# One threshold for two tiles, earlier weights for the first batch, a start split on GpSimd, and more transposes by DMA, in an attention kernel with a dense layer behind it

## The chip, the cores and the metric

The kernel runs on one core of a Trainium2 chip. The metric is the device time of one execution in microseconds (us), the median of several runs. All runs told here are on one core. Ratios are the mean time of one kernel's runs over that of the other kernel's runs of the same rounds, so not quite the ratio of the medians that are quoted beside them. The interval after a ratio holds it with 95%.

## The reference

Eight batches of eight heads, 576 positions, head size 64. Each head keeps only the scores within tau of its row's maximum, applies a softmax to them and multiplies by v. The heads are put side by side (512 columns) and go through a dense layer.

```python
scores = scale * np.matmul(q, k.transpose(0, 1, 3, 2))
thresh = np.max(scores, axis=-1, keepdims=True) - tau
scores = np.where(scores >= thresh, scores, -1000000000.0)
...                                     # softmax over the row
attn_out = np.matmul(attn, v)
x = attn_out.transpose(0, 2, 1, 3).reshape(B * S, H * D)
h = x @ w_in                            # 512 -> 2048
y = (h - np.tanh(h)) @ w_out            # 2048 -> 512
```

## The kernel before

Two heads make a pair; 32 pairs, of nine tiles of 128 query rows each (tile 4 is a mixed one, with 64 rows of either head, called M). The kernel walks over 288 slots, one tile a slot (about 1.6 us each in the steady part). In slot s it makes the scores of tile s+7, the threshold of tile s+6 (`shift`), the mask of tile s+5 (`kink`, on ScalarE), the weights of tile s (`weights`, an exp on ScalarE) and the product with v of tile s-2. TensorE also carries the dense layer of the previous batch between the slots. The mask `z` has to be transposed before the exp. In the first two batches TensorE does that, afterwards a DMA transpose does (`dma_start_transpose`; "by DMA" below), with two tiles in one transfer. All DMAs of the steady part are issued in order by one queue, that of SyncE (SP). q and k have to be turned too, by TensorE for every pair.

```python
AHEAD, MASK, LAG = 7, 5, 2
NPE = 2 * HPAIR * TPP                    # tiles transposed on TensorE
sc_pool = pool("sc", AHEAD - MASK + 2)
...
def scores(i):
    ...                                  # eight matmuls into ps
    mx = st_pool.tile([P, 1], F32, name="mx", tag="mx")
    nc.vector.tensor_scalar(out=sc, in0=ps[:, lo : lo + S], scalar1=SC,
        scalar2=None, op0=ALU.mult, op1=ALU.max, accum_out=mx)

def shift(i):                            # the threshold of one tile
    nb = st_pool.tile([P, 1], F32, name="nb", tag="nb")
    nc.vector.tensor_scalar(out=nb, in0=mx, scalar1=-1.0, scalar2=tau,
                            op0=ALU.mult, op1=ALU.add)

def kink(i):                             # the mask, then its transpose
    nc.scalar.activation(out=z, in_=sc, func=ACT.Prelu, bias=nb,
                         scale=1.0, alpha=STEEP)
    if i < NPE:
        zts[i] = zt                      # TensorE will transpose it
    elif kd != "A":                      # A: first tile of two, B: second
        nc.sync.dma_start_transpose(out=zts[i][:, 0:n, :], in_=zt)
...
for s in range(-AHEAD, NTILE + LAG + 3):
    shift(s + AHEAD - 1); scores(s + AHEAD)      # (bounds left out)
    kink(s + MASK); weights(s)
    ...                                  # a share of the dense layer
    attend(s - LAG)
    for step in plan.pop(s, []): step()  # loads, splits, turns of later pairs
```

Of the kernel before, what the change touches and what calls it, by code (L numbers as in the profile page):

```python
# [18 lines left out]
def kernel(  # L19
# [34 lines left out]
    NPE = 2 * HPAIR * TPP  # L54
# [4 lines left out]
    MASK = 5  # L59
# [21 lines left out]
    for i in range(NV):  # L81
        vb = const.tile([P, 2, 6, D + 1], BF16, name=f"vb{i}")
        nc.gpsimd.memset(vb[:, :, 4:6, :], 0.0)
        nc.vector.memset(vb[:, :, 0:4, D : D + 1], 1.0)
        nc.vector.memset(vb[0:64, :, 4, D : D + 1], 1.0)
        nc.vector.memset(vb[64:P, :, 5, D : D + 1], 1.0)
        vbs.append(vb)
# [3 lines left out]
    for i in range(NM):  # L91
# [9 lines left out]
    fold = const.tile([P, 64], BF16, name="fold")  # L101
    nc.vector.tensor_tensor(
        out=fold, in0=ident_bf[:, 0:64], in1=ident_bf[:, 64:P], op=ALU.add
    )

# [82 lines left out]
    def split_first(t, part):  # L188
        cs = (slice(0, 5), slice(5, TPP))[part]
        r = raws[0, t][:, cs, :]  # L190
        if part == 0:
            hls[0, t] = hl_pool.tile([P, TPP, 2, D], FP16, name=f"{t}hl", tag=t)
        hl = hls[0, t][:, cs, :, :]
        nc.scalar.mul(out=hl[:, :, 0, :], in_=r, mul=QKSC)
        nc.vector.scalar_tensor_tensor(
            out=hl[:, :, 1, :], in0=r, scalar=QKSC, in1=hl[:, :, 0, :],
            op0=ALU.mult, op1=ALU.subtract,
        )
# [25 lines left out]

    def turn(p, t):
        hl = hls.pop((p, t))
        ps = ps_big.tile([P, W], FP16, name=f"ps_{t}", tag="big")
# [7 lines left out]
        if t == "k":  # L235
            sw = qk_pool.tile([P, W], FP16, name="kS", tag="ks")
            nc.gpsimd.tensor_copy(out=sw[0:D, :], in_=m[D:P, :])  # L237
            nc.gpsimd.tensor_copy(out=sw[D:P, :], in_=m[0:D, :])  # L238
            mats[p, "ks"] = sw
# [25 lines left out]
    scs, zs, zts, pts, ops = {}, {}, {}, {}, {}  # L265
# [5 lines left out]
    def scores(i):  # L271
# [6 lines left out]
        if j == 4:  # L278
            for n, kk in enumerate((kT, kS)):
                for dst, srcs in ((main, MAIN), (rem, REM)):  # L280
                    for hh in range(2):
                        nc.tensor.matmul(  # L282
                            out=ps[64 * hh : 64 * hh + 64, dst],
                            lhsT=qT[:, REM[hh]], rhs=kk[:, srcs[hh]],
                            start=(n == 0), stop=(n == 1),
                        )
        else:
# [9 lines left out]
        mx = st_pool.tile([P, 1], F32, name="mx", tag="mx")  # L297
        nc.vector.tensor_scalar(  # L298
            out=sc, in0=ps[:, lo : lo + S], scalar1=SC, scalar2=None,
            op0=ALU.mult, op1=ALU.max, accum_out=mx,  # L300
        )
        scs[i] = sc, mx

    def shift(i):
        sc, mx = scs[i]
        nb = st_pool.tile([P, 1], F32, name="nb", tag="nb")
        nc.vector.tensor_scalar(  # L307
            out=nb, in0=mx, scalar1=-1.0, scalar2=tau, op0=ALU.mult, op1=ALU.add
        )
        scs[i] = sc, nb  # L310

    def kink(i):
        sc, nb = scs.pop(i)
# [13 lines left out]
        if i < NPE:  # L327
# [6 lines left out]
    def weights(i):  # L334
# [4 lines left out]
        if i < NPE:  # L339
            z = zts.pop(i)  # L340
            ps = ps_y.tile([P, 5 * P], BF16, name="psZ", tag="y")
# [126 lines left out]
    def project(m, ms, part, ps, last):  # L468
        for n in range(4 * part, 4 * part + 4):
            nc.tensor.matmul(  # L470
                out=ps, lhsT=gs[m][:, n, ms * P : (ms + 1) * P],
                rhs=w_out_sb[:, n, :], start=(n == 0), stop=(n == DF_C - 1),
            )
        if part == 3:
            yo = y_pool.tile([P, d_model], F32, name="yo")
# [7 lines left out]
            else:  # L483
                for h in range(2):
                    b = 2 * ms + h
                    stores.append(
                        lambda b=b, h=h: nc.sync.dma_start(
                            out=out[b * S + MB : (b + 1) * S, :],
# [3 lines left out]

    def layers(m, tail):

        steps, cur = [], {}
# [8 lines left out]
        def y_step(ms, part):  # L504
            if part == 0:
                tag = ("y", "o")[ms % 2] if tail else "y"
                pl = {"y": ps_y, "o": ps_o}[tag]
                cur["y"] = pl.tile([P, d_model], F32, name="psY", tag=tag)
            project(m - 1, ms, part, cur["y"], tail and ms % 2)

        for a in range(16):
            if m < NMB:
                steps.append(lambda a=a: h_step(a))
            if m > 0:
                steps.append(lambda a=a: y_step(a // 4, a % 4))
        return steps

# [15 lines left out]
    def w_load(piece):  # L533
# [20 lines left out]
        (3, lambda p: turn(p, "q")),  # L554
# [4 lines left out]
    for p in range(1, NPAIR):  # L559
        first = TPP * p - AHEAD  # L560
        for d, f in PREP[3 if p == 1 else 0 :]:
            plan.setdefault(first - d, []).append(lambda p=p, f=f: f(p))

# [3 lines left out]
    for t in ("k", "q", "ks"):  # L567
        turn_first(t, 0)
    split_v(0)
# [5 lines left out]
    todo, stage = [], 0  # L575

    for at in sorted(plan):
        if at < -AHEAD:
            plan.setdefault(-AHEAD, []).extend(plan.pop(at))
    for s in range(-AHEAD, NTILE + LAG + 3):  # L580
# [10 lines left out]
        if s == 1 - AHEAD:  # L591
            for t in ("k", "q"):
                split_first(t, 1)
        if s == 2 - AHEAD:
            for t in ("k", "q", "ks"):
                turn_first(t, 1)
        if 0 <= s + MASK < NTILE:
            kink(s + MASK)
        bend()
        if 0 <= s < NTILE:  # L600
            weights(s)
            if todo:
# [3 lines left out]
                while todo and done >= 1:  # L606
                    todo.pop(0)()
                    done -= 1
        shrink()
# [3 lines left out]
        if 0 <= s - LAG < NTILE:  # L613
            attend(s - LAG)
            pp, jj = divmod(s - LAG, TPP)
            if jj == 4:
                norm(pp, 0)
            if jj == 8:
                norm(pp, 1)
        pp, jj = divmod(s - LAG, TPP)  # L620
        if jj == 1 and 0 < pp <= NPAIR:
            emit_x(pp - 1)
# [10 lines left out]
    while stage <= NMB:  # L633
# [45 lines left out]
```

## Time and profile before

| | before |
|---|---|
| median of 4 runs (first comparison) | 552.1 us (550.9 to 552.7) |
| median of the 11 runs beside each group of experiments | 551.6 us |
| profiled span | 549.4 us |
| busy share of TensorE, VectorE, ScalarE | 95%, 81%, 81% |
| ScalarE's wait for a transposed mask | none |

The exp of a transposed mask (`pT<-zT`) never found ScalarE (ACT) idle.

### The profile page before, as it was taken

The page shows a single profiled execution, that of the slowest core. Times are in us where ns is not written, and L with a number is a line of the kernel's source. Part 1 is how long each engine was busy: PE and PEld are TensorE (multiplying, and loading weights), DVE is VectorE, ACT ScalarE, POOL GpSimd, SP SyncE. Part 2 cuts the span into 40 slices and gives each one's busy share as a digit, 9 for nine tenths or more (in the row PEclk, how much of TensorE's full clock was granted, in tenths as well). Part 3 has the DMA queues.
Part 4 walks back from the last instruction along what each step waited for, and adds up shares of the span by engine and source line. Part 5 has one row for each costly group of instructions (what it writes and reads, how often), then busy time and mean ns, then how long its engine had stood idle before and what let it go on. Part 6 is the DMA issues. An engine that isn't in the chain of part 4 may idle for free.

```text
span 549.4 us, 13518 instructions
## 1 busy us (share of the span) xinstructions
PE 521.8 (95%) x4954; PEld 302.4 (55%) x4954; DVE 444.1 (81%) x1349; ACT 443.3 (81%) x640; POOL 286.5 (52%) x372
## 2 busy tenths in 40 slices
PE   5888999999999999999999999999999999999996
PEld 2566666665555555555555555555555555444442
DVE  5888988898988999898889898898989888544430
ACT  3999999899899898989888988989898989533320
POOL 6788977666556666556555655666665620000000
PEclk9999999999999999999999999999999999999999
DMA  6755644437879888889977798877878966310103
GB/s 168 216 183 146 205 125 145 128 74 157 161 153 172 178 181 160 169 171 170 186 174 173 165 182 164 167 180 179 163 169 171 185 87 144 66 39 38 40 38 78
DMA packets 183011, 80.33 MB, mean 146 GB/s; under 512 B 150688, under 2 KB 175264, under 8 KB 182944
## 3 DMA queue, kind: packets, MB, share of 16 engines
q1 hardware_dynamic: 182512, 79.17, 65.0%
q8 instruction: 39, 0.64, 0.5%
q10 hardware_dynamic: 432, 0.30, 0.2%
q14 instruction: 28, 0.23, 0.2%
HBM read 37.75 MB, written 9.44 MB: 86 GB/s over the span
## 4 chain that ended last, share of the span: by engine, by line
PE 72%; DVE 16%; ACT 8%; issue 2%; DMA 1%; SPq 0%; ACTq 0%; DVEq 0%
PE psY L470 20%; PE psH L444 18%; PE psS L292 15%; DVE sc L298 6%; PE psO L389 5%; ACT pT L352 4%; PE psS L282 3%; ACT z L324 3%; DVE g L463 3%; PE psHt L444 3%; PE ps_q L221 2%; PE ps_k L221 2%; PE psZ L343 2%; DVE yo L479 1%; DVE kT L233 1%
## 5 line engine op out<-in xcount | busy, mean ns | idle before, releaser
L298 DVE TENSOR_SCALAR_CACHE_REDUCE sc<-psS 128x576 f32<-128x576 f32 x288 | 216.3, 751 | 19.8 <-PE psS L282 12.5
L324 ACT ACTIVATE z<-sc,nb 128x576 bf16<-128x576 f32 x256 | 195.7, 769 | 14.3 <-DVE nb L307 13.4
L470 PE MATMUL psY<-w_out_sb,g 128*128 128x512 bf16 x576 | 145.4, 379 | 0.0
L360 ACT ACTIVATE pT<-zT 128x1152 f16<-128x1152 bf16 (+1 forms) x120 | 127.8, 1065 | 0.0
L444 PE MATMUL psH<-xT,w_in_sb 128*128 128x512 bf16 x480 | 124.0, 379 | 0.3
L292 PE MATMUL psS<-kT,qT 128*128 128x512 f16 (+1 forms) x512 | 105.2, 287 | 10.1 <-DVE nb L307 7.6
L292 PEld LDWEIGHTS <-qT 128*128 128x128 f16 x1024 | 75.5, 98 | 68.1 <-issue 15.9
L237 POOL COPY kS<-kT 64x1152 f16<-64x1152 f16 x31 | 35.3, 1140 | 141.4 <-DVE nb L307 141.4
L463 DVE SCALAR_TENSOR_TENSOR g<-th,psH 128x512 bf16<-128x512 f32 x128 | 87.4, 683 | 22.0 <-ACT th L457 22.0
L292 PE MATMUL psS<-kS,qT 128*128 128x512 f16 x496 | 101.4, 286 | 0.0
L457 ACT ACTIVATE th<-psH 128x512 f32<-128x512 f32 x128 | 74.7, 584 | 17.8 <-PE psH L444 17.6
L470 PEld LDWEIGHTS <-g 128*128 128x128 bf16 x576 | 49.6, 98 | 57.7 <-issue 2.6
L444 PEld LDWEIGHTS <-w_in_sb 128*128 128x128 bf16 x576 | 49.3, 98 | 55.0 <-issue 2.7
L389 PEld LDWEIGHTS <-pT 128*128 128x128 f16 x1280 | 55.6, 98 | 24.3 <-ACT pT L360 2.1
L389 PE MATMUL psO<-vb,pT 128*128 128x65 bf16 x1280 | 61.2, 193 | 0.6 <-ACT pT L360 0.6
L352 ACT ACTIVATE pT<-psZ 128x640 f16<-128x640 bf16 (+1 forms) x72 | 47.2, 656 | 6.9 <-PE psZ L343 6.2
L307 DVE TENSOR_SCALAR nb<-mx 128x1 f32<-128x1 f32 x288 | 42.6, 148 | 3.4
L324 ACT ACTIVATE zm<-sc,nb 128x576 bf16<-128x576 f32 x32 | 24.8, 774 | 23.1 <-DVE nb L307 23.1
L183 POOL TENSOR_TENSOR qhl<-xs,qhl 128x576 f16<-128x576 f32 x31 | 39.7, 1280 | 2.6
L183 POOL TENSOR_TENSOR khl<-xs,khl 128x576 f16<-128x576 f32 x31 | 39.7, 1279 | 2.6
L238 POOL COPY kS<-kT 64x1152 f16<-64x1152 f16 x31 | 35.4, 1142 | 1.3
L343 PE MATMUL psZ<-ident_bf,z 128*128 128x128 bf16 x288 | 26.5, 219 | 4.5 <-ACT pT L352 4.3
(72 smaller groups left out, 561.6 us busy)
## 6 DMA issues: line engine op xcount, KB each, us to landing
vraw<-in_v_dram SPq DMA_DIRECT2D x32, 256.0 KB, 3.5
out_dram<-yo SPq DMA_DIRECT2D x32, 256.0 KB, 2.6
kraw<-in_k_dram SPq DMA_DIRECT2D x31, 256.0 KB, 3.1
qraw<-in_q_dram SPq DMA_DIRECT2D x31, 256.0 KB, 3.2
wt<-in_moe_w_in_dram SPq DMA_DIRECT2D x8, 512.0 KB, 4.4
wt<-in_moe_w_out_dram SPq DMA_DIRECT2D x8, 512.0 KB, 3.9
vraw<-in_v_dram SPq DMA_DIRECT2D x64, 32.0 KB, 2.9
zT<-z SPq DMA_TRANSPOSE x96, 3.3
```

Source lines behind the costliest of these rows:

```text
L183: nc.gpsimd.tensor_tensor(out=hl[:, :, 1, :], in0=x, in1=hl[:, :, 0, :], op=ALU.subtract)
L292: nc.tensor.matmul(out=ps[:, dst], lhsT=lhs, rhs=kk[:, src], start=(n == 0), stop=(n == 1),)
L298: nc.vector.tensor_scalar(out=sc, in0=ps[:, lo : lo + S], scalar1=SC, scalar2=None, op0=ALU.mult, op1=ALU.max, accum_out=mx,)
L307: nc.vector.tensor_scalar(out=nb, in0=mx, scalar1=-1.0, scalar2=tau, op0=ALU.mult, op1=ALU.add)
L324: nc.scalar.activation(out=z, in_=sc, func=ACT.Prelu, bias=nb, scale=1.0, alpha=STEEP)
L352: nc.scalar.activation(out=pt[:, off * P : (off + n) * P], in_=ps[:, 0 : n * P], func=ACT.Exp)
L360: nc.scalar.activation(out=pt[:, 0 : n * P], in_=zts.pop(i)[:, 0:n, :], func=ACT.Exp)
L389: nc.tensor.matmul(out=po[:, (j - 1 - 5 * hh) + ab, :], lhsT=pt[:, blk * P : (blk + 1) * P], rhs=vb[:, hh, c, :], start=(n == 0), stop=(n ...
L444: nc.tensor.matmul(out=ps, lhsT=w_in_sb[:, c, n * P : (n + 1) * P], rhs=xs[m][:, c, :] if m < B else xR[:, c, :, :], start=(c == 0), stop= ...
L457: nc.scalar.activation(out=th, in_=ps, func=ACT.Tanh)
L463: nc.vector.scalar_tensor_tensor(out=gs[m][:, n, :], in0=th, scalar=-1.0, in1=ps, op0=ALU.mult, op1=ALU.add,)
L470: nc.tensor.matmul(out=ps, lhsT=gs[m][:, n, ms * P : (ms + 1) * P], rhs=w_out_sb[:, n, :], start=(n == 0), stop=(n == DF_C - 1),)
```

## The change

Its intent: take transposes off TensorE, which bounds the steady part (58.2 of 59.2 us busy in a stage), and shorten both ends of the run. It has six parts: (1) q of twelve odd pairs goes by DMA; (2) in the second batch half of the masks go by DMA; (3) one threshold instruction serves two tiles, and so the mask comes one slot later (`MASK` 4); (4) the first batch's weights come three slots sooner; (5) at the start, GpSimd splits the second half of k and q; (6) the layer steps are reordered, and the last columns are stored in halves. `MASK` 4 also gives the scores one more buffer (`sc_pool` above). Beside the six, the diff holds small moves: a few `memset`s on GpSimd, the first four masks and the turns of pair 1 at other slots, a second bank for the first batch's transposes, and q by DMA issued five slots ahead in place of three. The core of the diff, shortened:

```diff
-    NPE = 2 * HPAIR * TPP
+    def on_pe(i):
+        p, j = divmod(i, TPP)
+        return p < HPAIR or p < 2 * HPAIR and j in (0, 1, 4, 5, 6)
-    MASK = 5
+    MASK = 4
@@ split_first: the second half of k and q on GpSimd
+        else:
+            nc.gpsimd.tensor_scalar(out=r, in0=r, scalar1=QKSC, ...)
+            nc.gpsimd.tensor_copy(out=hl[:, :, 0, :], in_=r)
+            nc.gpsimd.tensor_tensor(out=hl[:, :, 1, :], in0=r, in1=hl[:, :, 0, :], op=ALU.subtract)
@@ turn
+    def q_by_dma(p):
+        return p >= 2 * HPAIR and p % 2 == 1
+        if t == "q" and q_by_dma(p):
+            m = mats[p, t] = qk_pool.tile([P, W], FP16, name=f"{t}T", tag=t)
+            nc.sync.dma_start_transpose(out=m.rearrange(...), in_=hl.rearrange(...))
+            return
@@ shift: one threshold for two tiles
-        nb = st_pool.tile([P, 1], F32, name="nb", tag="nb")
+        if kd == "A":
+            return
+        n = 2 if kd == "B" else 1
+        nb = st_pool.tile([P, 2], F32, name="nb", tag="nb")
         nc.vector.tensor_scalar(
-            out=nb, in0=mx, scalar1=-1.0, scalar2=tau, op0=ALU.mult, op1=ALU.add
+            out=nb[:, 0:n], in0=mx[:, 0:n], scalar1=-1.0, scalar2=tau,
+            op0=ALU.mult, op1=ALU.add,
@@ the loop: weights and products of the first batch three slots sooner
+        at = i - 3 if i < HPAIR * TPP else i
...                     (layer order, halves of the last columns: cut)
```

More of the change, by code (lines that the diff above doesn't have):

```diff
@@ L83 @@
         nc.gpsimd.memset(vb[:, :, 4:6, :], 0.0)
-        nc.vector.memset(vb[:, :, 0:4, D : D + 1], 1.0)
-        nc.vector.memset(vb[0:64, :, 4, D : D + 1], 1.0)
-        nc.vector.memset(vb[64:P, :, 5, D : D + 1], 1.0)
+        nc.gpsimd.memset(vb[:, :, 0:4, D : D + 1], 1.0)
+        nc.gpsimd.memset(vb[0:64, :, 4, D : D + 1], 1.0)
+        nc.gpsimd.memset(vb[64:P, :, 5, D : D + 1], 1.0)
         vbs.append(vb)
@@ L100 @@
     nc.vector.memset(own[64:P, 1, :], 1.0)
-    fold = const.tile([P, 64], BF16, name="fold")
-    nc.vector.tensor_tensor(
-        out=fold, in0=ident_bf[:, 0:64], in1=ident_bf[:, 64:P], op=ALU.add
-    )
     pool = lambda name, bufs, **kw: ctx.enter_context(
@@ L193, in split_first @@
         hl = hls[0, t][:, cs, :, :]
-        nc.scalar.mul(out=hl[:, :, 0, :], in_=r, mul=QKSC)
-        nc.vector.scalar_tensor_tensor(
-            out=hl[:, :, 1, :], in0=r, scalar=QKSC, in1=hl[:, :, 0, :],
-            op0=ALU.mult, op1=ALU.subtract,
-        )
+        if part == 0:
+            nc.scalar.mul(out=hl[:, :, 0, :], in_=r, mul=QKSC)
+            nc.vector.scalar_tensor_tensor(
+                out=hl[:, :, 1, :], in0=r, scalar=QKSC, in1=hl[:, :, 0, :],
+                op0=ALU.mult, op1=ALU.subtract,
+            )
+        else:
+            nc.gpsimd.tensor_scalar(
+                out=r, in0=r, scalar1=QKSC, scalar2=1.0, op0=ALU.mult, op1=ALU.mult
+            )
+            nc.gpsimd.tensor_copy(out=hl[:, :, 0, :], in_=r)
+            nc.gpsimd.tensor_tensor(
+                out=hl[:, :, 1, :], in0=r, in1=hl[:, :, 0, :], op=ALU.subtract
+            )
     def split_v(p):
@@ L223, in turn_chunk @@
         )
+    def q_by_dma(p):
+        return p >= 2 * HPAIR and p % 2 == 1
     def turn(p, t):
         hl = hls.pop((p, t))
+        if t == "q" and q_by_dma(p):
+            m = mats[p, t] = qk_pool.tile([P, W], FP16, name=f"{t}T", tag=t)
+            nc.sync.dma_start_transpose(
+                out=m.rearrange("p (c r) -> p c r", c=TPP),
+                in_=hl.rearrange("p c a d -> p (c a d)"),
+            )
+            return
         ps = ps_big.tile([P, W], FP16, name=f"ps_{t}", tag="big")
@@ L236, in turn @@
             sw = qk_pool.tile([P, W], FP16, name="kS", tag="ks")
-            nc.gpsimd.tensor_copy(out=sw[0:D, :], in_=m[D:P, :])
-            nc.gpsimd.tensor_copy(out=sw[D:P, :], in_=m[0:D, :])
+            for lo, hi in ((0, D), (D, 0)):
+                o, i = sw[lo : lo + D, :], m[hi : hi + D, :]
+                nc.gpsimd.tensor_copy(out=o, in_=i)
             mats[p, "ks"] = sw
@@ L264 @@
     REM = (slice(512, 576), slice(576, 640))
-    scs, zs, zts, pts, ops = {}, {}, {}, {}, {}
+    scs, mxs, nbs, zs, zts, pts, ops = {}, {}, {}, {}, {}, {}, {}
     def kind(j):
@@ L278, in scores @@
         if j == 4:
+            qrem = REM
+            if q_by_dma(p):
+                qrem = (slice(512, 640, 2), slice(513, 640, 2))
             for n, kk in enumerate((kT, kS)):
@@ L283, in scores @@
                             out=ps[64 * hh : 64 * hh + 64, dst],
-                            lhsT=qT[:, REM[hh]], rhs=kk[:, srcs[hh]],
+                            lhsT=qT[:, qrem[hh]], rhs=kk[:, srcs[hh]],
                             start=(n == 0), stop=(n == 1),
@@ L296, in scores @@
         sc = sc_pool.tile([P, S], F32, name="sc")
-        mx = st_pool.tile([P, 1], F32, name="mx", tag="mx")
+        if kind(j) == "B":
+            mx = mxs[i] = mxs.pop(i - 1)
+        else:
+            mx = mxs[i] = st_pool.tile([P, 2], F32, name="mx", tag="mx")
+        c = int(kind(j) == "B")
         nc.vector.tensor_scalar(
             out=sc, in0=ps[:, lo : lo + S], scalar1=SC, scalar2=None,
-            op0=ALU.mult, op1=ALU.max, accum_out=mx,
+            op0=ALU.mult, op1=ALU.max, accum_out=mx[:, c : c + 1],
         )
-        scs[i] = sc, mx
+        scs[i] = sc
     def shift(i):
-        sc, mx = scs[i]
-        nb = st_pool.tile([P, 1], F32, name="nb", tag="nb")
+        kd = kind(i % TPP)
+        if kd == "A":
+            return
+        n = 2 if kd == "B" else 1
+        mx = mxs.pop(i)
+        nb = st_pool.tile([P, 2], F32, name="nb", tag="nb")
         nc.vector.tensor_scalar(
-            out=nb, in0=mx, scalar1=-1.0, scalar2=tau, op0=ALU.mult, op1=ALU.add
-        )
-        scs[i] = sc, nb
+            out=nb[:, 0:n], in0=mx[:, 0:n], scalar1=-1.0, scalar2=tau,
+            op0=ALU.mult, op1=ALU.add,
+        )
+        nbs[i] = nb[:, n - 1 : n]
+        if kd == "B":
+            nbs[i - 1] = nb[:, 0:1]
     def kink(i):
-        sc, nb = scs.pop(i)
+        sc, nb = scs.pop(i), nbs.pop(i)
         kd = kind(i % TPP)
@@ L326, in kink @@
         )
-        if i < NPE:
+        if on_pe(i):
             zts[i] = zt
@@ L338, in weights @@
         n, off = {"A": (4, 0), "M": (5, 0), "B": (5, 4)}[kd]
-        if i < NPE:
+        if on_pe(i):
             z = zts.pop(i)
-            ps = ps_y.tile([P, 5 * P], BF16, name="psZ", tag="y")
+            pl, tag = (ps_h, "h") if i % 2 and i < HPAIR * TPP else (ps_y, "y")
+            ps = pl.tile([P, 5 * P], BF16, name="psZ", tag=tag)
             for c in range(n):
@@ L466, in shrink, with project @@
             )
-    def project(m, ms, part, ps, last):
+    def project(m, ms, part, ps, last, cols=slice(0, d_model)):
         for n in range(4 * part, 4 * part + 4):
@@ L471, in project @@
                 out=ps, lhsT=gs[m][:, n, ms * P : (ms + 1) * P],
-                rhs=w_out_sb[:, n, :], start=(n == 0), stop=(n == DF_C - 1),
+                rhs=w_out_sb[:, n, cols], start=(n == 0), stop=(n == DF_C - 1),
             )
         if part == 3:
-            yo = y_pool.tile([P, d_model], F32, name="yo")
+            nc_ = cols.stop - cols.start
+            yo = y_pool.tile([P, nc_], F32, name="yo")
             if last:
@@ L485, in project @@
                     b = 2 * ms + h
+                    eng = nc.scalar if h and nc_ < d_model else nc.sync
                     stores.append(
-                        lambda b=b, h=h: nc.sync.dma_start(
-                            out=out[b * S + MB : (b + 1) * S, :],
+                        lambda b=b, h=h, eng=eng: eng.dma_start(
+                            out=out[b * S + MB : (b + 1) * S, cols],
                             in_=yo[64 * h : 64 * h + 64, :],
@@ L491, in project @@
                     )
+    EARLY = lambda m: 3 if m else 0
+    LAST = 1
+    quarters = lambda m: [(m, ms, part) for ms in range(4) for part in range(4)]
     def layers(m, tail):
-        steps, cur = [], {}
         def h_step(n):
@@ L502, in h_step, with y_step, y_half, ready @@
             hidden(m, n, ps)
-        def y_step(ms, part):
+        def y_step(m, ms, part):
             if part == 0:
-                tag = ("y", "o")[ms % 2] if tail else "y"
-                pl = {"y": ps_y, "o": ps_o}[tag]
-                cur["y"] = pl.tile([P, d_model], F32, name="psY", tag=tag)
-            project(m - 1, ms, part, cur["y"], tail and ms % 2)
-        for a in range(16):
-            if m < NMB:
-                steps.append(lambda a=a: h_step(a))
-            if m > 0:
-                steps.append(lambda a=a: y_step(a // 4, a % 4))
+                odd = ms % 2
+                pl, tag = (ps_o, "o") if tail and odd else (ps_y, "y")
+                ys[m, ms] = pl.tile([P, d_model], F32, name="psY", tag=tag), odd
+            ps, odd = ys[m, ms]
+            project(m, ms, part, ps, tail and odd)
+        def y_half(h):
+            n = d_model // 2
+            pl, tag = ((ps_y, "y"), (ps_o, "o"))[1 - h]
+            ps = pl.tile([P, n], F32, name="psY", tag=tag)
+            for part in range(4):
+                project(m, 3, part, ps, h == 0, slice(h * n, h * n + n))
+        now = quarters(m - 1)[EARLY(m - 1) :] if m > 0 else []
+        if m < NMB - 1:
+            now += quarters(m)[: EARLY(m)]
+        else:
+            now += quarters(m)[:12]
+        n = 16 + len(now)
+        ahead = n - max(0, EARLY(m) - 3) - LAST if m < NMB - 1 else n - 9 - LAST
+        steps, at, i = [], [], 0
+        def ready(y):
+            last = 4 * y[2] + 3
+            return y[0] < m or len(at) > last and at[last] + 2 < i
+        while now or len(at) < 16:
+            if len(at) < 16 and (
+                not now or not ready(now[0]) or len(at) * ahead <= i * 16
+            ):
+                steps.append(lambda a=len(at): h_step(a))
+                at.append(i)
+            elif ready(now[0]):
+                steps.append(lambda y=now.pop(0): y_step(*y))
+            else:
+                steps.append(lambda: None)
+            i += 1
+        if m == NMB - 1:
+            steps += [lambda h=h: y_half(h) for h in range(2)]
         return steps
+    ys = {}
     def w_pieces():
@@ L553 @@
         (5, lambda p: turn(p, "k")),
-        (3, lambda p: turn(p, "q")),
         (4, split_v),
@@ L561 @@
         for d, f in PREP[3 if p == 1 else 0 :]:
+            d -= p == 1 and d in (3, 5)
             plan.setdefault(first - d, []).append(lambda p=p, f=f: f(p))
+        d = 5 if q_by_dma(p) else 3 - (p == 1)
+        plan.setdefault(first - d, []).append(lambda p=p: turn(p, "q"))
     load(0, "v")
@@ L568 @@
         turn_first(t, 0)
+    for t in ("k", "q"):
+        split_first(t, 1)
     split_v(0)
@@ L575 @@
     todo, stage = [], 0
+    fold = const.tile([P, 64], BF16, name="fold")
     for at in sorted(plan):
@@ L579 @@
             plan.setdefault(-AHEAD, []).extend(plan.pop(at))
+    kinks, wts, atts = {}, {}, {}
+    for i in range(NTILE + 3):
+        at = i - 3 if i < HPAIR * TPP else i
+        atts.setdefault(at + LAG, []).append(i)
+        if i < NTILE:
+            wts.setdefault(at, []).append(i)
+            kinks.setdefault(i // 2 * 2 + 2 - AHEAD if i < 4 else i - MASK, []).append(i)
     for s in range(-AHEAD, NTILE + LAG + 3):
@@ L591 @@
         if s == 1 - AHEAD:
-            for t in ("k", "q"):
-                split_first(t, 1)
-        if s == 2 - AHEAD:
             for t in ("k", "q", "ks"):
                 turn_first(t, 1)
-        if 0 <= s + MASK < NTILE:
-            kink(s + MASK)
+        for i in kinks.pop(s, []):
+            kink(i)
         bend()
+        for i in wts.pop(s, []):
+            weights(i)
         if 0 <= s < NTILE:
-            weights(s)
             if todo:
@@ L608 @@
                     done -= 1
+        if s == 0:
+            nc.vector.tensor_tensor(
+                out=fold, in0=ident_bf[:, 0:64], in1=ident_bf[:, 64:P], op=ALU.add
+            )
         shrink()
@@ L612 @@
         del stores[:-1]
-        if 0 <= s - LAG < NTILE:
-            attend(s - LAG)
-            pp, jj = divmod(s - LAG, TPP)
-            if jj == 4:
-                norm(pp, 0)
-            if jj == 8:
-                norm(pp, 1)
-        pp, jj = divmod(s - LAG, TPP)
-        if jj == 1 and 0 < pp <= NPAIR:
-            emit_x(pp - 1)
+        for i in atts.pop(s, []):
+            pp, jj = divmod(i, TPP)
+            if i < NTILE:
+                attend(i)
+            if i < NTILE and jj in (4, 8):
+                norm(pp, int(jj > 4))
+            if jj == 1 and pp:
+                emit_x(pp - 1)
         for step in plan.pop(s, []):
@@ L631 @@
                     w_load(piece)
-    while stage <= NMB:
+    while stage < NMB:
         for step in layers(stage, True):
```

## The prediction

> **What bounds the kernel now.** I read four views in this order: the page's busy rows, the busy time cut into stages, the timeline of TensorE inside one stage, and the waits. The page first:
>
> ```profile
> PE 521.8 (95%) x4954; PEld 302.4 (55%) x4954; DVE 444.1 (81%) x1349; ACT 443.3 (81%) x640; POOL 286.5 (52%) x372
> ...
> PE   5888999999999999999999999999999999999996
> ...
> ACT  3999999899899898989888988989898989533320
> POOL 6788977666556666556555655666665620000000
> ```
>
> TensorE (PE) looks saturated, but its first four slices are not, and there ACT and GpSimd (POOL) are as full. So I cut the run where the hidden layer of a new batch begins (59.2 us apart in the steady part):
>
> ```profile
> core 0: us, PE busy (x) PEld busy (x) DVE busy (x) ACT busy (x) POOL busy (x), PEclk, DMA share, GB/s
> 0.00:14.00 14.00, 7.54 (x60) 4.05 (x61) 7.20 (x35) 5.68 (x11) 8.66 (x21) 1.00 0.62 171
> 14.00:73.50 59.50, 52.15 (x693) 37.27 (x690) 52.45 (x176) 55.95 (x90) 52.08 (x65) 1.00 0.62 189
> 73.50:130.20 56.70, 53.49 (x633) 35.25 (x632) 49.76 (x155) 51.62 (x84) 40.86 (x51) 1.00 0.41 111
> 130.20:189.40 59.20, 58.27 (x563) 33.50 (x562) 53.43 (x165) 52.56 (x72) 34.13 (x45) 1.00 0.83 167
> ...
> 476.00:544.80 68.80, 68.79 (x319) 30.98 (x317) 26.10 (x40) 22.04 (x37) 0.00 (x0) 1.00 0.13 43
> ```
>
> Four regimes: start and first batch (0 to 73.5, ACT 94% and POOL 88% after 14 us), second batch (73.5 to 130.2, ACT 91%, PE 94%), steady batches (130.2 to 476, PE 98%, DVE and ACT about 90%, DMA over 80%), dense tail (PE without a gap). PE's durations overlap, so I checked by starts:
>
> ```profile
> 182.36 0.48 PE L389 MATMUL psO<-vb,pT 128*128 128x65 bf16 x10
> 182.68 0.67 PE L221 MATMUL ps_q<-ident_f,qhl 128*128 128x128 f16 x9
> 183.18 0.41 PE L292 MATMUL psS<-kT,qT 128*128 128x512 f16 x2
> 183.42 0.41 PE L292 MATMUL psS<-kS,qT 128*128 128x512 f16 x2
> 184.57 0.41 PE L292 MATMUL psS<-kT,qT 128*128 128x512 f16 x2 [0.74 <-DVE nb L307]
> ```
>
> Nine transposes of q occupy PE for 183.18 - 182.68 = 0.50 us, a score tile for 2 x 0.24 = 0.49 us, a four-matmul layer step 0.86 us (starts in the chain). One pair of heads adds up to 9 score tiles 4.6, k and q turns 1.0, attention 1.6, x 0.25, 8 layer steps 6.9 = 14.35 us, against 59.2 / 4 = 14.8 measured. So in the steady part PE is the bound and only some 0.45 us a pair is gap. The gaps are the last line's sort: at the batch boundary four slots carry no layer work, VectorE sets the pace, and PE waits for a score bank (1.5 us a batch by my count of the timeline from 183.7 to 188).
>
> [...] The trace has 1.28 us for the 128x576 subtraction and 0.66 for the copy. [...] The trace has 3.3 us median from issue to landing, 5.5 at most, and 1.3 us of the SP queue for each issue.
>
> **The change part by part.**
>
> (1) q of 12 odd pairs from pair 9 on goes by DMA. PE loses 12 x 0.50 = 6.0 us; DVE loses 12 copies of 0.75. Of each two in a batch, one (the pair after the first) is turned just at the boundary where DVE sets the pace, so there it is the copy that counts, not PE's half microsecond. About the same size: 6 to 7 us in all, all on the path, because the steady part is bound at both places. The stage's DMA share of 0.85 rises: non-transposing traffic (0.9 MB loads plus 0.26 MB stores a pair) ran at about 290 GB/s per full share in the first batch (145 GB/s at 0.50), so it takes 0.27 of 0.85 and the 4.5 transposes a pair 0.58; one more on each second pair adds 0.06, to about 0.93 in the shorter stage.
>
> (2) Pairs 4 to 7: half the head blocks by DMA. 8 blocks x 9 transposes x 56 ns = 4.0 us off PE. ACT's exp of 0.60 + 0.70 becomes one of 1.15, which by starts is equal (1.07 against 1.06). So the stage falls from 56.7 towards ACT's 51.6 busy; with 1.5 us of the old stalls left, 53.2: 3.5 us gained.
>
> (3) The threshold instruction (nb) serves two tiles: 288 become 160. 128 x 0.148 = 19 us of DVE busy, but by starts one costs only 0.06 to 0.13, so about 12 us of a non-bounding engine. On the path only at the six batch boundaries, 3 instructions x 0.1 each: 1.5 us. Its price is that the mask comes one slot later (MASK 5 to 4), so a transpose has four slots instead of five to land. From issue to use are now 8.0 to 9.5 us (issue 201.24, exp at 210.72); less one slot of 1.6 leaves 6.4, still above 5.5.
>
> (4) First batch: weights three slots sooner, two banks for their transposes. ACT waits 0.2 to 0.5 us, two or three times a pair, for the single transpose bank. By starts ACT needs 10.9 us a pair and takes 12.05. But POOL needs 9.1 (splits, swapped k, v) + 2.25 weight casts x 1.01 = 11.4, so the pair can fall only to about 11.5: four pairs, 2 us.
>
> (5) Start: second half of k and q split by POOL. ACT's first z is at 13.50, after waiting for a split that DVE did at 10.81, behind the score tiles. On POOL each costs about 1.25 us (256 of 576 columns of 0.67 + 0.66 + 1.28, plus fixed parts), done near 8.5; z could start near 12. The score tiles then bind, so 1 us; POOL is 2.5 us later in the first batch, where it is nearly the bound. I count 0.5.
>
> (6) Layer order: three early y steps per stage move PE work between PE-bound stages: 0. Last columns in two halves, two queues: the end after the last matmul is 549.4 - 544.8 = 4.6; a copy of half size (0.4 for 0.59) and no second issue behind the first (0.5) give 0.7.
>
> Sum: 6.5 + 3.5 + 1.5 + 2 + 0.5 + 0.7 = 14.7 us. I take off 0.5 for later landings. 552.6 - 14.2 = 538.4.
>
> **The rivals.** (a) The DMA becomes the bound: at 0.93 average, landings go beyond 6.4 us and ACT's exp, then PE's attention, wait. For it: slices at 9 already, and one SP queue that issues everything in order (5 transposes x 1.35 + 7 loads x 0.58 + a store of 0.53 = 11.3 us of issue in 14.8 a pair, 12.7 in odd pairs). Against: today no exp waits for a transpose at all. It would cost half of (1): 542 to 546. (b) ACT or DVE takes over: ACT is at 52.7 of 59.1 in the steady stage, so the stage could fall to about 54 before that; 58 is predicted. It binds only in the second batch and is in the sum. (c) POOL or the SP queue gates the start: weight loads wait up to 8.3 us on that queue for POOL's casts, and now transposes of pairs 4 to 7 stand behind them. Then (2) and (4) vanish: 543 to 545. (d) Better than I say: the start becomes ACT-bound without POOL's limit, 3 to 4 us more: 534.
>
> **Range and chances.** Centre 538.4; the removed PE work of parts 1 and 2 is certain and on a saturated engine, the start is the least sure. 8 times in 10 between 533 and 545. The 2% line is at 541.5, 3 us above the centre: faster by over 2%: 0.74; within: 0.24; slower: 0.02.
>
> **What would show it.** Steady stages of 57.7 to 58.2 instead of 59.2, with PE still at 98% and the nb gap at the boundary smaller; second batch 53 to 54; its start (first hidden step) near 71 instead of 73.5; tail after the last matmul under 4. DMA share 0.9 or more with no exp waiting for zT. Wrong if ACT shows waits for zT, if a stage stays at 59 although 108 transposes are gone, or if POOL is without idle from 5 to 70 us and the layers start at 73 or later.

## More of the kernel before

Beyond what the prediction shows, four lines of the page matter later. They are the chain that ended last, two groups of ScalarE and the threshold of VectorE (columns after the shapes: count, then busy us and mean ns of one, then idle time just before, and what ended it; DVE is VectorE, ACT is ScalarE, PE is TensorE and PEld its weight loads):

```profile
PE 72%; DVE 16%; ACT 8%; issue 2%; DMA 1%; SPq 0%; ACTq 0%; DVEq 0%
...
L324 ACT ACTIVATE z<-sc,nb 128x576 bf16<-128x576 f32 x256 | 195.7, 769 | 14.3 <-DVE nb L307 13.4
...
L360 ACT ACTIVATE pT<-zT 128x1152 f16<-128x1152 bf16 (+1 forms) x120 | 127.8, 1065 | 0.0
...
L307 DVE TENSOR_SCALAR nb<-mx 128x1 f32<-128x1 f32 x288 | 42.6, 148 | 3.4
```

## The result, and the profile after

The changed kernel takes 555.5 us (4 runs, 555.1 to 557.3) against 552.1, ratio 1.0071 [1.0042, 1.0100]. It is slightly slower, well within 2%. The prediction was 538.4 with an upper end of 545, so it was wrong by 17 us. The page after, first the busy row, the slices and the chain:

```profile
PE 510.7 (92%) x4722; PEld 293.7 (53%) x4790; DVE 447.8 (81%) x1196; ACT 439.5 (79%) x630; POOL 290.1 (52%) x390
...
PE   5899789979999999998999899999999999899997
...
ACT  4999889888888888978998898878888899733330
...
PE 59%; DVE 16%; ACT 13%; DMA 7%; issue 5%; SPq 0%; ACTq 0%; DVEq 0%
```

TensorE lost 11.1 us of busy time, as it should with q and half a batch of masks taken away, yet the span grew by 4.1. Its share of the chain fell from 72% to 59%. ScalarE, DMA and "issue" took that over. DMA, 1% before, is now 7% of the path. The groups and the waits name the places; in the waits the numbers are us in total, times, and the longest:

```profile
L359 ACT ACTIVATE z<-sc,nb 128x576 bf16<-128x576 f32 x256 | 193.1, 768 | 21.4 <-DVE nb L339 20.8
L396 ACT ACTIVATE pT<-zT 128x1152 f16<-128x1152 bf16 (+1 forms) x128 | 137.4, 1074 | 16.5 <-DMA zT<-z 13.6
...
L339 DVE TENSOR_SCALAR nb<-mx 128x2 f32<-128x2 f32 (+1 forms) x160 | 49.1, 307 | 1.0
```

```profile
ACT pT L396 <- DMA zT<-z: 13.6, 12, 3.7
...
PEld L315 <- DMA qT<-qhl: 5.2, 8, 2.2
...
PE psS L315 <- DMA qT<-qhl: 2.8, 2, 2.1
```

Two things are new. ScalarE waits 13.6 us for masks to land, and TensorE waits for q. And the threshold, though there are 128 fewer of them, is busy longer in all (49.1 us against 42.6), because a two-column one takes 348 ns on average (151 to 999) where one column takes 143.

To see where the time went I cut both traces at the same work, the scores of the M tile of pairs 0, 4, 8 and so on, read off TensorE's timeline (us):

| | to pair 0 | 0 to 4 | 4 to 8 | 8 to 12 | 12 to 16 | 16 to 20 | 20 to 24 | 24 to 28 | 28 to 31 | rest |
|---|---|---|---|---|---|---|---|---|---|---|
| before | 13.4 | 47.6 | 56.6 | 59.8 | 59.2 | 59.2 | 59.2 | 59.2 | 43.9 | 91.4 |
| after | 12.0 | 46.0 | 57.1 | 62.5 | 60.4 | 62.2 | 60.6 | 60.0 | 43.8 | 89.0 |

The start and the first batch are shorter. In the third stage 2.6 us are merely moved: three y steps, 12 matmuls at 0.216, come from the rest. But the steady stages, which the prediction put at 57.7 to 58.2, grew by up to 3.0. One of them, as busy times of each engine, before and then after:

```profile
236.54:295.70 59.16, 58.23 (x563) 33.46 (x560) 53.31 (x164) 52.75 (x73) 34.46 (x44) 1.00 0.86 172
```

```profile
237.92:300.14 62.22, 58.11 (x537) 32.86 (x543) 53.22 (x146) 52.44 (x73) 34.46 (x44) 0.97 0.91 176
```

All engines show nearly the same busy time in 3 us more (the bracket counts instructions), so what was added is mostly gaps; in 3.4 us of this stage TensorE also ran at a granted clock of 0.50, of which more below. Now the gap itself, in the chain of that stage (start, length, what), followed by TensorE's timeline of the same moment:

```profile
244.70 0.69 ACT pT L396
245.39 5.40 DMA zT<-z
250.79 0.02 issue
```

```profile
248.80 1.03 PE L506 MATMUL psY<-w_out_sb,g 128*128 128x512 bf16 x4
252.12 0.63 PE L425 MATMUL psO<-vb,pT 128*128 128x65 bf16 x10 [2.29 <-ACT pT L396]
```

A transpose issued at 245.39 landed 5.40 us later. ScalarE had been ready for it since 247.18 (it waited 3.72), and TensorE then stood still for 2.29 us. The last view is of what GpSimd (POOL) does beside a threshold (nb), at 305.0 to 310.3 of the kernel after:

```profile
305.03 1.14 POOL L258 COPY kS<-kT 64x1152 f16<-64x1152 f16 x1
...
305.75 0.45 DVE L339 TENSOR_SCALAR nb<-mx 128x2 f32<-128x2 f32 x1
...
309.01 1.28 POOL L182 TENSOR_TENSOR khl<-xs,khl 128x576 f16<-128x576 f32 x1
...
309.95 0.36 DVE L339 TENSOR_SCALAR nb<-mx 128x2 f32<-128x2 f32 x1
```

The first threshold ends at 306.20 and the copy on GpSimd at 306.17; the second ends at 310.31 and the subtraction on GpSimd at 310.29. This holds throughout: in the change 68 of the 128 two-column thresholds take over 200 ns, and each of the 68 ends 21 to 27 ns after a GpSimd instruction does. The 42 that began while GpSimd was idle took 170 ns at most. In the kernel before, 191 of the one-column thresholds began while GpSimd was running, and none of the 288 took more than 156 ns.

### The profile page after: what moved, and what is told of

The parts are those of the page before. It is cut to its first block, busy times and chain, and to the rows that moved or that the text cites.

```text
span 553.5 us, 13009 instructions
## 1 busy us (share of the span) xinstructions
PE 510.7 (92%) x4722; PEld 293.7 (53%) x4790; DVE 447.8 (81%) x1196; ACT 439.5 (79%) x630; POOL 290.1 (52%) x390
## 4 chain that ended last, share of the span: by engine, by line
PE 59%; DVE 16%; ACT 13%; DMA 7%; issue 5%; SPq 0%; ACTq 0%; DVEq 0%
PE psY L506 17%; PE psH L480 14%; PE psS L315 14%; DVE sc L325 7%; ACT z L359 5%; PE psO L425 4%; ACT pT L396 3%; DMA zT<-z 3%; DVE g L499 3%; DMA qT<-qhl 2%; PE psHt L480 2%; ACT pT L388 2%; PE psS L305 2%; DVE nb L339 2%; PE ps_k L229 2%
## 5 line engine op out<-in xcount | busy, mean ns | idle before, releaser
L325 DVE TENSOR_SCALAR_CACHE_REDUCE sc<-psS 128x576 f32<-128x576 f32 x288 | 214.0, 750 | 20.9 <-PE psS L315 10.8
L359 ACT ACTIVATE z<-sc,nb 128x576 bf16<-128x576 f32 x256 | 193.1, 768 | 21.4 <-DVE nb L339 20.8
L396 ACT ACTIVATE pT<-zT 128x1152 f16<-128x1152 bf16 (+1 forms) x128 | 137.4, 1074 | 16.5 <-DMA zT<-z 13.6
L506 PE MATMUL psY<-w_out_sb,g 128*128 128x512 bf16 (+1 forms) x559 | 139.6, 373 | 2.3 <-issue 0.8
L480 PE MATMUL psH<-xT,w_in_sb 128*128 128x512 bf16 x447 | 118.5, 381 | 4.4 <-DVE g L499 2.8
L480 PEld LDWEIGHTS <-w_in_sb 128*128 128x128 bf16 x576 | 49.4, 98 | 59.2 <-issue 6.8
L339 DVE TENSOR_SCALAR nb<-mx 128x2 f32<-128x2 f32 (+1 forms) x160 | 49.1, 307 | 1.0
L388 ACT ACTIVATE pT<-psZ 128x640 f16<-128x640 bf16 (+1 forms) x56 | 36.6, 656 | 6.1 <-PE psZ L379 5.9
L516 DVE COPY yo<-psY 128x512 f32<-128x512 f32 (+1 forms) x31 | 21.1, 679 | 10.7 <-PE psY L506 6.7
L440 DVE TENSOR_TENSOR osb<-psO,rc 128x256 bf16<-128x256 f32 x64 | 27.2, 424 | 2.2
L229 PE MATMUL ps_k<-ident_f,khl 128*128 128x128 f16 x288 | 22.0, 221 | 5.3 <-DVE khl L195 5.3
```

Of the source, the lines that this page charges most:

```text
L339: nc.vector.tensor_scalar(out=nb[:, 0:n], in0=mx[:, 0:n], scalar1=-1.0, scalar2=tau, op0=ALU.mult, op1=ALU.add,)
L396: nc.scalar.activation(out=pt[:, 0 : n * P], in_=zts.pop(i)[:, 0:n, :], func=ACT.Exp)
L480: nc.tensor.matmul(out=ps, lhsT=w_in_sb[:, c, n * P : (n + 1) * P], rhs=xs[m][:, c, :] if m < B else xR[:, c, :, :], start=(c == 0), stop= ...
L506: nc.tensor.matmul(out=ps, lhsT=gs[m][:, n, ms * P : (ms + 1) * P], rhs=w_out_sb[:, n, cols], start=(n == 0), stop=(n == DF_C - 1),)
```

## The experiments

**The theory.** Part (3) is what failed, in two ways. A two-column threshold is stopped by GpSimd (348 ns on average, where one column takes 143), and a four-slot mask leaves too little time for transposes to land once q goes the same way. **Rivals.** The DMA is simply overloaded with transposes by parts (1) and (2), so that undoing either mends the kernel; or the merge of two thresholds costs by itself, because the first tile has to wait for the second. All kernels gave correct results, and each was timed in five rounds. In six of the fifteen runs the time missed every range that I had written down by about 1 us or more; this is said at each.

### First group: the change with one thing undone

Two one-column instructions in place of a two-column one:

```diff
-        nc.vector.tensor_scalar(out=nb[:, 0:n], in0=mx[:, 0:n], ...)
+        for c in range(n):
+            nc.vector.tensor_scalar(out=nb[:, c : c + 1], in0=mx[:, c : c + 1], ...)
```

> The changed kernel, but the threshold for two tiles is made by two one-column instructions at the same place instead of one of two columns. [...] (the two-column form, 348 ns mean and up to 999, waits for GpSimd's current instruction, the one-column form, 143 ns, does not): all 288 instructions have a mean near 145 ns, VectorE frees the score banks sooner, TensorE's waits for the score copy (8.7 us) shrink to 3 or less, and the time falls by 3 to 7 us to 549 to 552. Landing theory (only the late DMA transposes cost the steady batches): the mean falls too, but the time stays within 1.5 us of 555.5.

Measured: 553.0 us, ratio to the kernel before 1.0025 [1.0005, 1.0045]. All thresholds now take 142 to 157 ns, but the waits for masks rose from 13.6 to 22.6 us and those for q from 8.0 to 11.4. The time lies between the ranges of the two theories, and TensorE's waits for the score copy fell to 6.0 us only, not to 3. The stall is real, and only 2.5 us of it show in the time; the longer waits suggest that what is freed in front is lost at the next one.

q back on TensorE for all pairs:

```diff
-        return p >= 2 * HPAIR and p % 2 == 1
+        return False
```

> The changed kernel with every q turned by TensorE again. Landing theory (the 12 added transposes make the others and q itself late): waits for q (8 us) and for the weights' transposes (13.6 us on ScalarE) go to under 2 us, steady batches return to 59 to 59.5 us and the time falls by 3 to 6 us to 550 to 552.5. [...] the waits go but TensorE has 6 us more work and still waits for VectorE, so the time stays within 2 us of 555.5 or rises.

Measured: 552.6, ratio 1.0019 [1.0004, 1.0033]. The waits for masks fall from 13.6 to 2.5 us, those for q are gone, and the change is 2.9 us *faster* without the part that was to give it 6 to 7. It is still no faster than the kernel before.

The second batch back on TensorE:

```diff
-        return p < HPAIR or p < 2 * HPAIR and j in (0, 1, 4, 5, 6)
+        return p < 2 * HPAIR
```

> The changed kernel with the whole second batch transposed by TensorE again, as in the kernel before. If the mixed batch is a gain as predicted (TensorE relieved of 4 us), this run is 2 to 4 us slower than 555.5. If ScalarE's stalls at the change from DMA to TensorE blocks eat it, it is within 1 us or faster.

Measured: 552.5, ratio 1.0013 [0.9997, 1.0030]; waits for masks 9.9 us. The second stage kept its 57.4 us (57.1 with the part), so the 3 us are won elsewhere, above all from pair 16 to 20 (59.2 in place of 62.2), which the edit doesn't touch. Why is not shown. Inside the change, then, part (2) costs 3 us.

The five-slot mask with the merged threshold kept:

```diff
-    MASK = 4
+    MASK = 5
```

> The changed kernel with the mask made five slots ahead again, as in the kernel before, all else as changed: each transpose has a slot (1.6 us) more to land. Landing theory: ScalarE's waits for the weights' transposes (13.6 us) go to under 3 us, time falls by 2 to 5 us to 550.5 to 553.5. [...] within 1.5 us of 555.5, because the masks then wait more for the threshold.

Measured: 577.7, ratio 1.047. This was a miss, and my own mistake. With the merge, the first tile's threshold is made in slot s for tile s+5, which is the very slot of its mask. ScalarE then waited 62.2 us for thresholds (20.8 in the change). The waits for masks did fall, to 0.4 us. So the run shows that merge and five slots exclude each other, not what a slot is worth.

### Second group: single parts on the kernel before, and part (3) undone whole

Only q of odd pairs by DMA, on the kernel before (the edit is the `turn` part of the diff above, with the slot of its issue and the order of its rows in the M tile):

> The kernel before with one part alone: q of the odd pairs from 9 on by DMA (mask still five slots ahead, one threshold per tile). Slack theory (q by DMA is a gain of 6 us of TensorE work that only the shortened landing time of the changed kernel loses): ScalarE waits less than 3 us for transposes, steady batches 57.8 to 58.4 instead of 59.2, time 545 to 548. Saturation theory (the DMA engines, at 0.85 before, can't take 12 more transposes in time whatever the slack): waits of over 8 us appear, steady batches 59 or longer, time 550.5 to 554.

Measured: 545.3, ratio 0.9886 [0.9873, 0.9899]: 6.3 us gained, with 2.1 us of waits for masks and none for q. Part (1) gives what was predicted (6 to 7) when it stands alone, and the DMA isn't overloaded by it.

Only the merged threshold with `MASK` 4, on the kernel before:

> The kernel before with one part alone: the two-column threshold for two tiles, and the mask four slots ahead that it brings. [...] the two-column form has a mean near 0.35 us, VectorE is not relieved, the first two batches lose 1 to 3 us, and the time is 552.5 to 556. My prediction's count (128 instructions fewer): 549 to 551.

Measured: 558.5, ratio 1.0129 [1.0115, 1.0144]: 6.9 us *lost*, where the prediction has a gain of 1.5, and more than either range allowed. With no q transposed by DMA the waits for masks are only 3.0 us, so here it is the threshold itself.

Part (3) undone in the change, threshold per tile and `MASK` 5:

```diff
-    MASK = 4
+    MASK = 5
@@ shift: as in the kernel before, one column, no merge
```

> The changed kernel with the threshold per tile and the mask five slots ahead again, as before the change; all else changed. Slack theory: waits for the weights' transposes under 4 us, steady batches 58 to 59, time 545 to 549. Saturation theory: waits stay over 8 us, time 551 to 554.

Measured: 541.9, ratio 0.9821 [0.9808, 0.9833]. This is 13.6 us faster than the change, and 9.7 faster than the kernel before; I had expected 545 at best. TensorE's waits for q are down from 8.0 to 1.5 us, the waits for masks to 2.2 (4 of them, 0.9 at most):

```profile
ACT pT L384 <- DMA zT<-z: 2.2, 4, 0.9
```

One-column thresholds and q on TensorE, both in the change:

> The changed kernel with one-column thresholds and every q turned by TensorE: both repairs that each gave 2.5 to 3 us. If they repair different losses (VectorE's in the first two batches, landing in the steady ones) they add: 549 to 551. If they are the same loss seen twice: 552 to 553.

Measured: 547.1, ratio 0.9923 [0.9909, 0.9936]. Against the run with q on TensorE and two columns (552.6), the form costs 5.5 us where there are fewer waits for landings (5.7 us here); in the change it cost 2.5. The time is below both ranges.

### Third group: part (3) taken apart

`MASK` 4 alone, on the kernel before:

> The kernel before with the mask four slots ahead and nothing else. If the later slot itself is the loss (transposes land too late, weights wait): 554 to 557, most of the 6.9 us that the two-column threshold with it cost. If the loss is that the first tile's threshold waits for the second tile[...]: 551 to 552.5.

Measured: 551.5, ratio 0.9994 [0.9982, 1.0006]. There a slot less costs nothing (the 3.3 us of waits for masks don't show in the time).

The merge and `MASK` 4 on the kernel before, but two one-column instructions:

> The kernel before with the mask four slots ahead and the two thresholds made together, but by two one-column instructions. [...] the wait for GpSimd is gone, so 2 to 4 us less than the two-column form's 558.5: 554.5 to 556.5. [...]

Measured: 550.3, ratio 0.9980 [0.9968, 0.9992]. Against 558.5 the two-column form costs 8.2 us, and making both thresholds together gains about one. So the prediction's -1.5 would have been nearly right for this form. The time is 4 us below the range that I gave for a stop by GpSimd (554.5 to 556.5), and further below that for a stop off the path (557.5 to 559): I had put the form at 2 to 4 us.

The change with a threshold per tile and `MASK` 4:

> The changed kernel with thresholds per tile, each one slot after its scores, and the mask kept four slots ahead. Slot theory (the later mask is what costs): ScalarE waits over 8 us for transposes and the time is 549 to 553, near the 553.0 of the one-column pair. Hold theory (the threshold held back for the second tile is what costs): 542 to 545, near the 541.9 with five slots.

Measured: 549.0 with a wide spread (546.9 to 554.2), ratio 0.9963 [0.9929, 0.9997]. Its waits for masks:

```profile
ACT pT L384 <- DMA zT<-z: 20.7, 20, 3.3
```

That is nine times those of the five-slot kernel. From 541.9 to here is 7.1 us for the slot that cost nothing before. From here to the one-column merge (553.0) is about 4, for holding the first tile's threshold until the second's; by the two intervals that can be 0.4 to 6.4.

Part (3) undone, and the second batch all on TensorE:

> The changed kernel with threshold per tile and five slots, and the second batch all by TensorE. If my prediction's part on the second batch holds once the slots are back (TensorE relieved of 4 us): 544.5 to 546, with the second batch 2.5 to 4 us longer. If ScalarE paces that batch in both forms: 541 to 543.

Measured: 542.2, ratio 0.9832 [0.9820, 0.9845]. Part (2) is worth 0.3 us, which is within the noise, and not 3.5.

### Fourth group: the two causes, and the layer order

The kernel with the merge on the kernel before (558.5), but the threshold in a form that also writes an accumulator. The score copies have such a form in every kernel (`accum_out`): in the change the 288 of them took 739 to 759 ns, although 191 began while GpSimd was running. That a threshold in this form isn't stopped either is what I expected, and no run before this one had shown it. The test keeps the merge and the columns:

```diff
@@ scores (out and in0 cut)
-            ... scalar1=SC, scalar2=None, op0=ALU.mult, op1=ALU.max, accum_out=mx[:, c : c + 1],
+            ... scalar1=-SC, scalar2=None, op0=ALU.mult, op1=ALU.min, accum_out=mx[:, c : c + 1],
@@ shift
-            out=nb[:, 0:n], in0=mx[:, 0:n], scalar1=-1.0, scalar2=tau, op0=ALU.mult, op1=ALU.add
+            out=nb[:, 0:n], in0=mx[:, 0:n], scalar1=tau, scalar2=None, op0=ALU.add,
+            op1=ALU.min, accum_out=nb[:, 2:3]
@@ kink
-            out=z, in_=sc, func=ACT.Prelu, bias=nb, scale=1.0, alpha=STEEP
+            out=z, in_=sc, func=ACT.Prelu, bias=nb, scale=-1.0, alpha=STEEP
```

> The kernel before with the merged two-column threshold and a four-slot mask, as in the run that measured 558.5, but the threshold instruction also writes an accumulator [...]; the sign is moved into the scale of the mask so that the result stays right. Theory [...]: no threshold over 0.3 us any more, and the time falls to that of the two one-column instructions, 550.3, plus at most 2 us for the accumulator: 550 to 553. Rival (the merge itself, or two columns as such, costs the 8 us): the long tail of durations stays (maximum near 1.3 us) and the time stays 557 to 560.

Measured: 550.6, ratio 0.9974 [0.9960, 0.9988]. The groups of the threshold, first with the plain two-column form, then with one column twice, then with the accumulator:

```profile
L316 DVE TENSOR_SCALAR nb<-mx 128x2 f32<-128x2 f32 x128 | 42.0, 328 | 0.7
```

```profile
L317 DVE TENSOR_SCALAR nb<-mx 128x1 f32<-128x1 f32 x288 | 32.2, 145 | 0.0
```

```profile
L316 DVE TENSOR_SCALAR_CACHE_REDUCE nb<-mx 128x2 f32<-128x2 f32 x128 | 18.8, 147 | 0.7
...
L316 DVE DVE_READ_ACCUMULATOR nb<-mx 128x1 f32 x160 | 13.2, 83 | 0.0
```

The mean falls from 328 to 147 ns with the same merge and the same two columns, and the longest of all from 1274 to 156 ns. The whole 8 us come back, with an extra 13.2 us of accumulator reads on VectorE. The rival (the merge, or two columns as such) falls for the kernel before. What is left is the form that can be stopped by GpSimd: in the plain form each of the 63 thresholds over 200 ns ends 22 to 27 ns after a GpSimd instruction, and with the accumulator none is over 200 ns, although 85 of the 128 began while GpSimd was running.

q of every pair from pair 8 on by DMA, part (3) undone:

> The change with one threshold per tile and a five-slot mask (541.9), and q of every pair from 8 on [...], 12 more 128x1152 transposes. If DMA has room left: another 12 x 0.50 us off TensorE, 535 to 538, with ScalarE's exp waiting under 6 us for transposed masks. If DMA is at its limit: waits for transposed masks of 15 us or more and no gain, 541 to 548. I lean to the second, since steady slices already show 9 and 10 tenths.

Measured: 542.3, ratio 0.9827 [0.9803, 0.9851], no gain over 541.9, with 10.8 us of waits for masks, fewer than the 15 or more I expected.

The layer order of before, part (3) undone:

> The same kernel (541.9) with the layer order of before: no early steps, last columns in one piece. The prediction gave the early steps 0 and the last columns 0.7. So 542.0 to 543.2, with the third stage 2.6 us shorter and the part after the last pair 2.6 to 3.3 longer. Rival: the early steps fill gaps of the second layer stage, then 544 or more.

Measured: 541.4, ratio 0.9809 [0.9792, 0.9826]. The last part is 91.4 us against 88.6 and the third stage 58.7 against 60.9, so the early steps move work and nothing else. It is not distinguishable from 541.9, though it has the lowest median of all versions that were run.

### Is it the landing time or the room for it?

The median from issue to landing hardly moved (3.3 us before and after; the longest 5.5 and 5.9). So I counted the room that each transpose has: from the start of its issue to the moment at which ScalarE is free for its exp, by pairing the issues on the SP queue with the exps in order, in one profiled execution of each kernel.

| kernel | median room, us | least | exps with under 4 us | waits for masks, us |
|---|---|---|---|---|
| before | 7.4 | 4.1 | 0 of 120 | 0 |
| before, `MASK` 4 | 5.3 | 3.3 | 11 of 120 | 3.3 |
| before, q of odd pairs by DMA | 6.0 | 2.9 | 11 of 120 | 2.1 |
| the change | 5.2 | 1.7 | 28 of 128 | 13.6 |
| the change, q on TensorE | 5.4 | 3.2 | 10 of 128 | 2.5 |
| the change, a threshold per tile, `MASK` 4 | 5.1 | 1.8 | 36 of 128 | 20.7 |
| the same, `MASK` 5 | 7.2 | 3.0 | 9 of 128 | 2.2 |
| the same, q of all later pairs by DMA | 5.8 | 2.0 | 28 of 128 | 10.8 |

The two parts eat the same room. A slot less takes 2.0 us off the median, and the twelve transposes of q, on the same queue, take 1.3. Each alone leaves about a dozen exps under 4 us and costs ScalarE 2 to 3 us of waiting; together they leave 28 to 36, and 14 to 21 us. In the change, slices of half a microsecond around the long wait of the result section show one thing more (columns: window, length, busy times, the granted clock, DMA share, GB/s):

```profile
249.00:249.50 0.50, 0.50 (x4) 0.20 (x2) 0.41 (x1) 0.00 (x0) 0.43 (x1) 1.00 0.00 0
249.50:250.00 0.50, 0.33 (x2) 0.00 (x0) 0.49 (x3) 0.00 (x0) 0.48 (x1) 1.00 0.05 4
250.00:250.50 0.50, 0.00 (x0) 0.00 (x0) 0.50 (x1) 0.00 (x0) 0.50 (x1) 1.00 0.08 10
...
252.50:253.00 0.50, 0.50 (x7) 0.26 (x6) 0.00 (x0) 0.50 (x2) 0.00 (x0) 0.50 0.00 0
253.00:253.50 0.50, 0.50 (x6) 0.23 (x4) 0.00 (x0) 0.50 (x2) 0.00 (x0) 0.50 0.00 0
```

While ScalarE waits for the mask, the DMA moves 0 to 10 GB/s for 1.5 us. A full queue of data isn't what it waits for here, although the stage's mean share is 0.91. What the DMA does in that stretch no run tells. After TensorE's 2.29 us of standing still, its granted clock is 0.50 for 3.4 us (252.3 to 255.7), which by my estimate (the missing share of the clock in each half microsecond) makes up at most 1.7 of the 3.0 us of this stage. What lowered it isn't shown: after a stop of 2.12 us at 122.5 in the same execution the clock stays at 1.00. It doesn't explain the slower kernel: runs of the change with a mean clock of 1.000 and of 0.996 took 555.6 and 555.4 us.

## Why the prediction was wrong, point by point

**The step that failed is part (3)**, "The threshold instruction (nb) serves two tiles ... 1.5 us. Its price is that the mask comes one slot later". It was put at -1.5 us. Measured, it is +6.9 alone and +13.6 inside the change; taken off one after the other there, the two-column form gives 2.5, the hold of the first tile's threshold about 4 and the slot 7.1. Without part (3) the prediction's sum would be 552.6 - 12.7 = 539.9, and the kernel without it takes 541.9. That these are so near is partly luck: part (2) was put 3.2 us too high, and parts (4) and (5) together some 1.5 too low. The gain of 1.5 itself was a slip, as six boundaries of three instructions at 0.1 make 1.8. Three things were missed in part (3):

- *The form.* "by starts one costs only 0.06 to 0.13" was read from one column and carried over to two. Shown: 328 ns in place of 145, 8.2 us on the kernel before, and it comes back whole in the form with the accumulator (147 ns). That GpSimd is what stops it is seen in the ends, all within 0.03 us of a GpSimd instruction's, and in the thresholds that began while GpSimd was idle (170 ns at most). No run took GpSimd's work away.
- *The room.* "From issue to use are now 8.0 to 9.5 us ...; less one slot of 1.6 leaves 6.4" was read at one place, where the room is large (8.0 or more for 43 of 120). Over all 120 transposes the median was 7.4 and the least 4.1. The step compared the largest room with the longest landing, where it needed the least. Shown: 7.1 us for the slot in the change (549.0 to 541.9), 0 in the kernel before (551.5 to 551.6).
- *The sum.* Parts (1) and (3) were added as if independent, but both draw on that room. In the change, putting q on TensorE gains 2.9 us; on the kernel before, taking it off gains 6.3.

The remaining 4 us or so, the first tile's threshold held for the second, are not settled: the intervals are wide, and the same hold costs nothing on the kernel before.

**Part (1)** was right: -6 to -7 predicted, -6.3 alone. **Part (2)** was right in that TensorE loses the transposes, and wrong in size: 0.3 in place of 3.5. The second stage takes 56.1 us with the part and 56.5 without, both close to the 56.6 of before. The removed 4.0 us of TensorE are not what paces it; I took ScalarE's 51.6 busy as the floor and didn't ask what fills the other 5. What does isn't shown. **Parts (4) and (5)** were right in direction and put too low: the first batch is 3.0 and the start 0.8 to 1.1 us shorter (stages of 541.4 and 541.9) against 2 and 0.5. The limit that I saw in GpSimd, 11.5 us a pair, was too tight (44.6 / 4 = 11.1). No run takes these two parts, or the small moves beside them, off alone. **Part (6)**: the order was 0 as predicted. The last columns show 0.2 us at most (91.4 of before against 88.6 plus the 2.6 moved) in place of 0.7, and the whole kernel shows nothing.

**The rivals.** Rival (a), "landings go beyond 6.4 us and ACT's exp, then PE's attention, wait", saw the symptom and gave it 542 to 546. Its cause, a DMA that becomes the bound, isn't what the runs show: no landing of a mask took more than 5.9 us, and the waits fall to 2.2 us with one slot more and all twelve q still transposed by DMA. With 24 of them the room shrinks again, and the landings don't get longer (5.2 at most). Rival (c) said that parts (2) and (4) would vanish: (2) did, for a reason that isn't shown, and (4) didn't. The sign I gave for being wrong, "if ACT shows waits for zT, if a stage stays at 59 although 108 transposes are gone", is what came.

## What to carry to other kernels

Before taking a slot away from a prefetch, list the room of every transfer and look at the smallest values; and where two parts of a change draw on the same room, don't add their gains. An instruction that is made wider can be stopped where the narrow one wasn't (328 ns in place of 145 on the kernel before): a tiny VectorE instruction in the path of other engines is better left in a form that GpSimd doesn't stop, here one column (145 ns) or the accumulator (147). When a bundle gives nothing, undo its parts one at a time and also put each on the old kernel alone: here that found one bad part in six, and versions at 541.4 to 541.9 us, 1.8 to 1.9% faster than the kernel before.
